# Sums of the second batch by identity matmuls, its inputs fetched a head pair sooner, and the first p_val queued behind the first batch's last o_l

## The chip, the cores and the metric

The kernel runs on one core of one Trainium2 chip, in one launch. The metric is the device time of one execution in microseconds (us), median of the runs shown. TensorE is PE in the profile (its weight loads PEld), VectorE is DVE, ScalarE is ACT, GpSimd is POOL, SyncE is SP; SP issues all DMAs here.

## The reference

Four batches go through attention, a gated convolution block and a mixer block, all in float32. Cut to what matters:

```python
# attention: B, H, S, D = 4, 8, 576, 64; factor 4
q_d = q.reshape(B, H, S // 4, 4, D).mean(axis=3)      # the same for k and v
out_up = np.repeat(softmax(q_d @ k_d.T / 8) @ v_d, 4, axis=2)
out_local = softmax(where(|i - j| < 4, q @ k.T / 8, -1e9)) @ v
x = out_up + out_local                                # (B, S, 512) over the heads
# gated convolution
gate = sigmoid(sum_k conv_w[k] * x shifted by 4 - k positions)
x = (gate * (x @ w_val)) @ w_out
# mixer
u = x + (relu(x.T @ w_tok1) @ w_tok2).T
out = u + relu(u @ w_ch1) @ w_ch2                     # w_ch1: 512 x 1536, w_ch2: 1536 x 512
```

## The kernel before

Everything is held transposed: channels on the 128 partitions, positions along the free axis. A head pair is 128 channels (two heads of 64), so a batch has four head pairs (NHP = 4), and x has four such chunks.

**Attention of a batch** (`attention(b)`) is a generator. For each head pair it runs these steps: `load` (DMAs of q and k into `qk_sb` and of v, four positions apart, into `v4_sb`, which the profile calls v_sb of in_v), `sums` (the sums of four positions: `qk_d` for q and k, `vd` for v), `low_scores` (scores `sc_d` of the sums, and the softmax `e_d`), `loc_scores` (scores `sc_l` of windows of 64 positions, softmax `e_l`), `low_turn` and `low_out` (transposes `pt_d`, products `o_d`, which ACT repeats into `x_f`), `loc_turn` and `loc_out` (transposes `pt_l`, products `o_l`, which DVE adds to `x_f`), and `conv` (the convolution on DVE). There are two buffers for `qk_sb`; one comes free when the `sc_l` matmuls of its head pair are done.

`sums` has two forms. In batch 0, four PE matmuls with the identity as weights add up the four positions in PSUM (each takes every fourth column, 288 of them, in plain float32; the profile records each as two MATMULs), and ACT copies the sum to SBUF. In the other batches one DVE reduction does it.

**The rest of a batch** is `p1(b)`: x is split into a high and a low part (`x_hl`: ACT makes the high part, POOL the low one), every large product is three matmuls (`mm3`, lines 194 to 196: high by high, high by low, low by high). `val` makes `p_val` = x @ w_val, one 128-channel chunk per bank, `outs` makes `p_x`, `transposed` the transposes `x_ps`, then `r_ps`, `p_h` (both tok products) and at last `u_hl`. `c1(b)` makes `g_ps` = u @ w_ch1, and ACT's relu `r_sb` goes to DRAM. `c2` reads it back at the end and makes `p_o` with w_ch2.

The weights come as pairs of 32-bit words and are decoded on the way: three DVE instructions per piece (`decode`, lines 124 to 127, buffers `w64` and `wa`, three each), a high part on ACT and a low one on POOL.

**Order.** Batch 0's attention runs first, with idle matmuls (`busy`, line 108) between its steps. There the framework's scheduler sets the order on all engines. From then on PE's order is written out by hand: `mix` runs `first_products` (p1 and c1 of all batches) and takes a step of the next batch's attention or of a weight's decoding after so many microseconds of planned PE time (`A_AT`: batch 1 from 8 to 59). The other engines' order remains the scheduler's, by program order and priority. Each engine then goes through its own list in order, and waits at the first instruction that isn't ready.

Of the kernel before, what the change touches and what calls it, by code (L numbers as in the profile page):

```python
# [21 lines left out]
NHP = H // 2  # L22
# [52 lines left out]
def kernel(ctx, tc, qk, vw, v4, w_val, conv_w, w_out, w_tok1, w_tok2, w_ch1, w_ch2, out):  # L75
    nc = tc.nc
# [5 lines left out]
    def T(p, shape, dt, tag, bufs, name=None):  # L82
        return p.tile(shape, dt, tag=tag, bufs=bufs, name=name or tag)
# [113 lines left out]


    xf, gate = {}, {}
    LU = [(0, 6), (6, 10)]  # L200

    def load(b, hp):

        early = b == 0 and hp > 1
        t = T(sb, [128, 2, PADW], F32, "uhl" if early else "qk", NUH if early else 2, name="qk_sb")
        nc.sync.dma_start(out=t, in_=qk[b, hp])
        tag, bufs = ("x2r", NX2) if b == 0 and hp > 0 else ("v4", NV4)
        w = T(sb, [72, 4, 2, 128], F32, tag, bufs, name="v4_sb")
        nc.sync.dma_start(out=w, in_=v4[b, hp])
        return {"qk": t, "v4": w, "v": load_v(b, hp) if b == 0 else None}  # L210

    def load_v(b, hp):
        tag, bufs = ("w1", NW1R) if b == 0 and hp > 1 else ("v", NV)
        v = T(sb, [128, NCK // 2, 128], F32, tag, bufs, name="v_sb")
        nc.sync.dma_start(out=v, in_=vw[b, hp])
        return v
# [24 lines left out]
    def attention(b):  # L241
        x_t = xf[b] = [T(sb, [128, CQ * NCK], F32, "xf", NXF, name="x_f32") for _ in range(KC)]
        g_t = gate[b] = [T(sb, [128, S], F32, "gate", NXF, name="gate_sb") for _ in range(KC)]
        hpd = {}
        early = lambda: tc.high_priority(offset=PRI) if b else nullcontext()

        def bank(shape, name):
            if b:
                tag = "as" if name[:2] == "sc" else "ao"
            else:  # L250
                tag = TAG0.get(name, "ao")
            return T(ps, shape, F32, tag, BANKS[tag], name=name)

        def sums(hp):
            d = hpd[hp]
            w = d.pop("v4")
            qk_d = T(sb, [128, 2, SD], F32, "qkd", ND, name="qk_d")
            qd, kd = qk_d[:, 0], qk_d[:, 1]
            qk_4 = d["qk"][:, :, 3:3 + S].rearrange("p i (a r) -> p i a r", r=4)
            if b == 0:  # L260
                p = bank([128, 2, SD], "qk_d")
                for r in range(4):
                    nc.tensor.matmul(p, lhsT=ident, rhs=qk_4[:, :, :, r], start=(r == 0), stop=(r == 3))
                nc.scalar.activation(out=qk_d, in_=p, func=AF.Copy)
            else:
                nc.vector.tensor_reduce(out=qk_d, in_=qk_4, axis=AX.X, op=ALU.add)
            vd = d["vd"] = T(sb, [72, 2, 128], F32, "vd", NVD, name="vd")
            nc.gpsimd.tensor_tensor(out=w[:, 0:2], in0=w[:, 0:2], in1=w[:, 2:4], op=ALU.add)
            nc.gpsimd.tensor_tensor(out=vd, in0=w[:, 0], in1=w[:, 1], op=ALU.add)
            d["qkd"] = qd, kd  # L270

        def low_scores(hp):
            d = hpd[hp]
            qd, kd = d.pop("qkd")
            parts = [bank([72, 2, SD], "sc_d") for _ in range(2)]
            for c in range(2):
                for h, p in enumerate(parts):
                    r0 = 64 * h
                    nc.tensor.matmul(p[:, c, :], lhsT=qd[r0:r0 + 64, c * HD:c * HD + HD],
                                     rhs=kd[r0:r0 + 64, :], start=True, stop=True)  # L280
            e = d["ed"] = T(sb, [72, 4, SD], F32, "e", NE, name="e_d")
            softmax(parts, e, 0.125 / 16.0)

        def low_turn(hp):
            d = hpd[hp]
            e = d.pop("ed")
            ts = d["pd"] = []
            for h in range(2):
                p = bank([72, 2, 2, HD], "pt_d")
                for kc in range(2):  # L290
                    for c in range(2):
                        nc.tensor.transpose(p[:, kc, c, :], e[:, 2 * h + c, kc * HD:kc * HD + HD], ident[0:72, 0:72])
                t = T(sb, [72, 2, 2, HD], F32, "pt", NPT, name="pts_d")
                with early():
                    nc.scalar.activation(out=t, in_=p, func=AF.Copy)
                ts.append(t)
# [15 lines left out]
        def loc_scores(hp):  # L312
            d = hpd[hp]
            qk = d.pop("qk")
            parts = []
            for c0, c1 in LU:
                n = c1 - c0
                p = bank([128, n, WIN], "sc_l")
                nc.tensor.matmul(p.rearrange("p a w -> p (a w)"), lhsT=ident16,
                                 rhs=mask[:, c0:c1, :].rearrange("p a w -> p (a w)"), start=True, stop=False)  # L320
                for c in range(n):
                    o = CQ * (c0 + c)
                    for h in range(2):
                        r0 = 64 * h
                        nc.tensor.matmul(p[r0:r0 + 64, c, :], lhsT=qk[r0:r0 + 64, 0, 3 + o:3 + o + WIN],  # L325
                                         rhs=qk[r0:r0 + 64, 1, o:o + WIN], start=False, stop=(c == n - 1))
                parts.append(p)
            e = d["el"] = T(sb, [128, NCK, WIN], F32, "e", NE, name="e_l")
            softmax(parts, e, 0.125)

        def loc_turn(hp):
            d = hpd[hp]
            e = d.pop("el")
            ts = d["pl"] = []
            for c0, c1 in LU:
                n = (c1 - c0) // 2
# [9 lines left out]
        def loc_out(hp):  # L346
            d = hpd.pop(hp)
            v, ts = d["v"], d["pl"]
            ps_o = [bank([128, NCK // 2, CQ], "o_l") for _ in range(2)]
            for j, t in enumerate(ts):  # L350
                for par in range(2):
                    r0 = 64 * par
                    for h in range(2):
                        nc.tensor.matmul(ps_o[par][64 * h:64 * h + 64, j, :],
                                         lhsT=v[r0:r0 + 64, j, 64 * h:64 * h + 64],
                                         rhs=t[r0:r0 + 64, 64 * h:64 * h + CQ], start=True, stop=True)
            xs = x_t[hp].rearrange("p (j a q) -> p j a q", a=2, q=CQ)
            with early():
                for par in range(2):
                    nc.vector.tensor_tensor(out=xs[:, :, par, :], in0=ps_o[par], in1=xs[:, :, par, :], op=ALU.add)  # L360
# [12 lines left out]
        def sigmoid(s0=0, s1=S):  # L373
            for g in g_t:
                nc.scalar.activation(out=g[:, s0:s1], in_=g[:, s0:s1], func=AF.Sigmoid)

        if b:

            hpd[0] = load(b, 0)
            hpd[0]["v"] = load_v(b, 0)  # L380
            yield
            sums(0)
            for i in range(NHP + 1):
                if i < NHP:
                    low_scores(i)
                    yield
                if i:
                    low_turn(i - 1)
                    yield
                if i < NHP:  # L390
                    loc_scores(i)
                    yield
                if i + 1 < NHP:
                    hpd[i + 1] = load(b, i + 1)
                    sums(i + 1)
                if i:
                    low_out(i - 1)
                    yield
                    loc_turn(i - 1)
                    yield  # L400
                    loc_out(i - 1)
                    conv(i - 1)
                    yield
                if i + 1 < NHP:
                    hpd[i + 1]["v"] = load_v(b, i + 1)
            sigmoid()
            return
# [42 lines left out]
    def hv(hs):  # L450
        return slice(hs * HS, hs * HS + HS)

    def bank(tag, name):
        return T(ps, [128, 512], F32, tag, BANKS[tag], name=name)

    def cxs(p, w, xs, c, ks=range(KC)):
        for k in ks:
            mm3(p[:, 0:HS], [w[k][j][:, c * 128:c * 128 + 128] for j in range(2)],
                [xs[j][:, k] for j in range(2)], k == 0, k == KC - 1)
# [3 lines left out]
    def p1(b):  # L463

        wv, wo, t1, t2 = wt["val"], wt["out"], wt["tok1"], wt["tok2"]
# [9 lines left out]

        def val(hs, c, x, y2):
            p = bank(P1T["p_val"], "p_val")
            cxs(p, wv, x, c)
            with first():
                y = T(sb, [128, HS], F32, "y32", NY, name="y32")  # L480
                nc.vector.tensor_tensor(out=y, in0=p[:, 0:HS], in1=gate[b][c][:, hv(hs)], op=ALU.mult)  # L481
                hi_lo(y, y2[0][:, c], y2[1][:, c], nc.gpsimd if b else nc.vector)
# [24 lines left out]
        x = x_pair(0)  # L507
# [4 lines left out]
        x = x_pair(1)  # L512
# [36 lines left out]
        for hs in range(2):  # L549
            us.append(pair("u", "uhl", NUH))  # L550
            for c in range(KC):
                p = bank(P1T["p_h"], "p_h")
# [170 lines left out]
```

## Time and profile before

| | |
|---|---|
| median of 3 runs | 666.46 us (664.31 to 666.83) |
| the profiled execution: time / span | 664.67 us / 662.8 us |
| PE busy | 622.3 us, 94% of the span |
| DVE, ACT, POOL busy | 339.4, 316.4, 210.0 us |
| mean granted TensorE clock | 0.972 of 2.4 GHz |

Busy time is a share of the whole span. Batch 0's attention fills the first 80 us or so, the second batch's runs beside batch 0's products from about 94 to 190 us, and roughly the last quarter of the span is w_ch2. The granted clock has two levels, 1.2 and 2.4 GHz; a mean between 0.5 and 1 says how long each held.

### The profile page before, as it was taken

The numbers are of one execution on the slowest core, as the hardware profiler recorded it, in microseconds if no ns is written. First come the engines' busy times: TensorE is split into PE (matmuls) and PEld (weight loads), VectorE is DVE, ScalarE is ACT, GpSimd is POOL, SyncE is SP. The second block draws the span as 40 slices with busy tenths as digits, with TensorE's granted clock in tenths as the row PEclk, the third lists the DMA queues.
The fourth block names the chain that finished last, engine by engine and source line by source line (L and its number), as shares of the span: only waits on it lengthen the run. The fifth ranks groups of instructions, "written<-read, shape, count | busy, mean of one in ns | idle before, by whom it ended". The sixth has DMA issues, their size and how long they took to land.

```text
span 662.8 us, 12825 instructions
## 1 busy us (share of the span) xinstructions
PE 622.3 (94%) x4911; PEld 529.6 (80%) x4911; DVE 339.4 (51%) x630; ACT 316.4 (48%) x1044; POOL 210.0 (32%) x242
## 2 busy tenths in 40 slices
PE   8999778897979999999999999999998999999997
PEld 3444477785878988998998999998897888888887
DVE  3679999775686465442344434117635242324232
ACT  1758457485548586546656843324433222222221
POOL 5564655336536422614231323205513000000000
PEclk8999798797979999999999999999999999999999
DMA  7744226623675244784322586565898345454221
GB/s 254 235 143 117 76 81 205 217 75 122 221 244 178 87 150 131 242 245 124 105 72 72 146 255 203 160 195 187 252 355 272 96 144 174 142 176 127 80 74 38
DMA packets 53900, 107.23 MB, mean 162 GB/s; under 512 B 5776, under 2 KB 21392, under 8 KB 53840
## 3 DMA queue, kind: packets, MB, share of 16 engines
q1 hardware_dynamic: 53840, 106.42, 51.1%
q8 instruction: 38, 0.62, 0.4%
q14 instruction: 22, 0.18, 0.1%
HBM read 76.52 MB, written 29.88 MB: 161 GB/s over the span
## 4 chain that ended last, share of the span: by engine, by line
PE 60%; DVE 6%; DMA 5%; ACT 3%; issue 2%; POOL 1%; SPq 0%; DVEq 0%; ACTq 0%
PE p_o L194 7%; PE p_o L196 7%; PE p_o L195 7%; PE g_ps L194 5%; PE g_ps L195 5%; PE g_ps L196 5%; DMA w<-in_w_ch_dram 4%; PE sc_l L325 2%; PE p_x L194 2%; DVE wa L124 2%; PE p_x L195 2%; PE p_x L196 2%; PE p_val L194 2%; PE p_val L196 2%; PE p_val L195 2%
## 5 line engine op out<-in xcount | busy, mean ns | idle before, releaser
L194 PE MATMUL g_ps<-u_hl,w_hl 128*128 128x288 f32 x384 | 117.8, 307 | 0.0
L195 PE MATMUL g_ps<-u_hl,w_hl 128*128 128x288 f32 x384 | 115.0, 299 | 2.1 <-POOL u_hl L444 1.9
L196 PE MATMUL g_ps<-u_hl,w_hl 128*128 128x288 f32 x384 | 113.9, 297 | 0.0
L194 PE MATMUL p_o<-g_hl,ch 128*128 128x512 f32 (+1 forms) x240 | 88.8, 370 | 2.2 <-ACT r_sb L585 2.1
L196 PE MATMUL p_o<-g_hl,ch 128*128 128x512 f32 (+1 forms) x240 | 88.5, 369 | 0.0
L195 PE MATMUL p_o<-g_hl,ch 128*128 128x512 f32 (+1 forms) x240 | 88.5, 369 | 0.0
L443 ACT ACTIVATE g_hl<-r_back 128x512 fp32r<-128x512 f32 (+1 forms) x60 | 35.3, 589 | 109.1 <-PE p_o L196 106.3
L444 DVE TENSOR_TENSOR g_hl<-r_back,g_hl 128x512 fp32r<-128x512 f32 (+1 forms) x60 | 39.4, 658 | 92.8 <-ACT g_hl L443 89.6
L195 PEld LDWEIGHTS g_ps<-u_hl,w_hl 128*128 128x128 f32 x384 | 73.3, 191 | 3.5 <-POOL u_hl L444 3.5
L194 PEld LDWEIGHTS g_ps<-u_hl,w_hl 128*128 128x128 f32 x384 | 73.1, 190 | 3.1 <-issue 1.7
L196 PEld LDWEIGHTS g_ps<-u_hl,w_hl 128*128 128x128 f32 x384 | 73.2, 191 | 0.0
L370 DVE SCALAR_TENSOR_TENSOR gate_sb<-x_f,cw,gate_sb 128x575 f32<-128x575 f32 (+5 forms) x68 | 62.8, 930 | 1.5 <-ACT gate_sb L367 0.5
L585 ACT ACTIVATE r_sb<-g_ps 128x288 f32<-128x288 f32 x96 | 38.2, 406 | 47.0 <-PE g_ps L196 41.2
L124 DVE TENSOR_SCALAR wa<-w 128x256 int32<-128x256 int32 (+2 forms) x76 | 37.1, 499 | 34.8 <-DMA w<-in_w_ch_dram 21.1
L194 PEld LDWEIGHTS p_o<-g_hl,ch 128*128 128x128 f32 x240 | 45.2, 188 | 10.8 <-ACT r_sb L585 3.2
L196 PEld LDWEIGHTS p_o<-g_hl,ch 128*128 128x128 f32 x240 | 45.2, 188 | 7.7
L195 PEld LDWEIGHTS p_o<-g_hl,ch 128*128 128x128 f32 x240 | 45.3, 189 | 7.6
L234 ACT ACTIVATE e_l<-sc_l,mx 128x64 f32<-128x64 f32 x160 | 48.1, 331 | 0.4
L194 PE MATMUL p_x<-y_hl,out_hi 128*128 128x288 f32 x128 | 40.9, 320 | 4.2 <-ACT u_sb L494 3.7
L125 DVE SCALAR_TENSOR_TENSOR wa<-w,wa 128x256 int32<-128x256 int32 (+2 forms) x76 | 44.2, 591 | 1.1
L444 POOL TENSOR_TENSOR x_hl<-x_f,x_hl 128x288 fp32r<-128x288 f32 x32 | 27.7, 877 | 45.5 <-ACT x_hl L443 44.8
L194 PE MATMUL p_val<-x_hl,val_hi 128*128 128x288 f32 x128 | 39.5, 309 | 1.4 <-DVE y L481 0.7
(108 smaller groups left out, 1354.0 us busy)
## 6 DMA issues: line engine op xcount, KB each, us to landing
w_hl<-w_dr SPq DMA_DIRECT2D x36, 512.0 KB, 4.6
r_dr<-r_sb SPq DMA_DIRECT2D x48, 288.0 KB, 4.6
w<-in_w_ch_dram SPq DMA_DIRECT2D x48, 256.0 KB, 3.4
r_back<-r_dr SPq DMA_DIRECT2D x48, 256.0 KB, 3.0
qk_sb<-in_qk_dram SPq DMA_DIRECT2D x16, 589.0 KB, 4.0
w_dr<-w_hl SPq DMA_DIRECT2D x12, 512.0 KB, 3.0
v_sb<-in_vw_dram SPq DMA_DIRECT2D x16, 320.0 KB, 4.0
v_sb<-in_v_dram SPq DMA_DIRECT2D x16, 288.0 KB
```

The lines of the kernel that those rows point to most:

```text
L124: nc.vector.tensor_scalar(a, high, 3, 0x3FFFFFF8, ALU.logical_shift_left, ALU.bitwise_and)
L125: nc.vector.scalar_tensor_tensor(out=a, in0=high, scalar=-0x40000000, in1=a, op0=ALU.bitwise_and, op1=ALU.bitwise_or)
L194: nc.tensor.matmul(out_ap, lhsT=lh, rhs=rh, start=first, stop=False)
L195: nc.tensor.matmul(out_ap, lhsT=lh, rhs=rl, start=False, stop=False)
L196: nc.tensor.matmul(out_ap, lhsT=ll, rhs=rh, start=False, stop=last)
L234: nc.scalar.activation(out=e[:, o, :], in_=p[:, c, :], func=AF.Exp, scale=scale, bias=mx[:, o:o + 1], accum_out=sm[:, o:o + 1])
L325: nc.tensor.matmul(p[r0:r0 + 64, c, :], lhsT=qk[r0:r0 + 64, 0, 3 + o:3 + o + WIN], rhs=qk[r0:r0 + 64, 1, o:o + WIN], start=False, stop=(c ...
L370: nc.vector.scalar_tensor_tensor(out=g[:, t0:s1], in0=x[:, t0 - sh:s1 - sh], scalar=cw[:, hp, k:k + 1], in1=g[:, t0:s1], op0=ALU.mult, op1 ...
L443: nc.scalar.activation(out=hi_ap, in_=src_ap, func=AF.Copy)
L444: lo_eng.tensor_tensor(out=lo_ap, in0=src_ap, in1=hi_ap.bitcast(F32), op=ALU.subtract)
L585: nc.scalar.activation(out=r[:, hv(hs)], in_=p[:, 0:HS], func=AF.Relu)
```

## The change

Three edits. `sums` takes the identity-matmul form for batch 1 too. Batch 1 loads two head pairs before its loop, and then the one after next behind `sums` of the next, where it loaded one ahead. And the first `p_val` chunk of batch 0 gets an order edge on PE: its matmuls are queued behind the last `o_l` matmul of batch 0's attention.

```diff
+    last_pe = [None]
...
-            if b == 0:
+            if b < 2:
                 p = bank([128, 2, SD], "qk_d")
                 for r in range(4):
                     nc.tensor.matmul(p, lhsT=ident, rhs=qk_4[:, :, :, r], start=(r == 0), stop=(r == 3))
                 nc.scalar.activation(out=qk_d, in_=p, func=AF.Copy)
             else:
                 nc.vector.tensor_reduce(out=qk_d, in_=qk_4, axis=AX.X, op=ALU.add)
...
-                        nc.tensor.matmul(ps_o[par][64 * h:64 * h + 64, j, :],
+                        last_pe[0] = nc.tensor.matmul(ps_o[par][64 * h:64 * h + 64, j, :],
...
-            hpd[0] = load(b, 0)
+            ahead = 2 if b == 1 else 1
+            for i in range(ahead):
+                hpd[i] = load(b, i)
...
+                if ahead == 1 and i + 1 < NHP:
+                    hpd[i + 1] = load(b, i + 1)
                 if i + 1 < NHP:
-                    hpd[i + 1] = load(b, i + 1)
                     sums(i + 1)
+                if ahead == 2 and i + 2 < NHP:
+                    hpd[i + 2] = load(b, i + 2)
...
-            cxs(p, wv, x, c)
+            with tc.issue_after(last_pe[0].ins) if b + hs + c == 0 else nullcontext():
+                cxs(p, wv, x, c)
```

What this does to the engines' lists is seen in three places. The first is PE's list at the last head pair of batch 0. Before, the first p_val (12 matmuls for one chunk) stood spread between the attention's steps, one chunk of x at a time:

```order
L292 MATMUL pt_d<-ident,e_d 72x72 x8
L194 MATMUL p_val<-x_hl,val_hi 128x288
L195 MATMUL p_val<-x_hl,val_hi 128x288
L306 MATMUL o_d<-pts_d,vd 64x144
L108 LDWEIGHTS idle
L108 MATMUL idle_ps<-idle 128x512
L196 MATMUL p_val<-x_hl,val_lo 128x288
```

Now the same place reads so:

```order
L293 MATMUL pt_d<-ident,e_d 72x72 x8
L307 MATMUL o_d<-pts_d,vd 64x144
L108 LDWEIGHTS idle
L108 MATMUL idle_ps<-idle 128x512
L108 LDWEIGHTS idle
L108 MATMUL idle_ps<-idle 128x512
```

Nine p_val matmuls (three of the four chunks of x) have left the attention's steps; all twelve follow the last o_l and its idle matmuls.

The second place is PE's list in batch 0's products, where the second batch's first head pair takes its turn. Before:

```order
L196 MATMUL p_x_1101<-y_hl,out_lo 128x288
L279 MATMUL sc_d<-qk_d 72x144 x4
L194 MATMUL p_x_1100<-y_hl,out_hi 128x288
L195 MATMUL p_x_1100<-y_hl,out_hi 128x288
L196 MATMUL p_x_1100<-y_hl,out_lo 128x288
```

Now:

```order
L196 MATMUL p_x_1101<-y_hl,out_lo 128x288
L264 MATMUL qk_d<-qk_sb,ident 128x288 x4
L280 MATMUL sc_d<-qk_d 72x144 x4
L194 MATMUL p_x_1100<-y_hl,out_hi 128x288
L195 MATMUL p_x_1100<-y_hl,out_hi 128x288
```

Four identity matmuls stand right ahead of the scores that read their sum by way of ACT. It is the same for the second head pair (between p_val and x_ps); those of the third and fourth stand ahead of the o_d of the head pair two before, with their scores some 50 matmuls later. The third one's, now (before, o_d followed p_x directly):

```order
L196 MATMUL p_x_1468<-y_hl,out_lo 128x288
L264 MATMUL qk_d<-qk_sb,ident 128x288 x4
L307 MATMUL o_d<-pts_d,vd 64x144 x4
L194 MATMUL p_x_1467<-y_hl,out_hi 128x288
L195 MATMUL p_x_1467<-y_hl,out_hi 128x288
```

Here o_d, and the p_x that follow it, wait for four more matmuls of PE's own, and nothing reads the sum at once.

The third place is SP's list, where the second batch's third head pair is fetched between the pieces of w_ch1. Before:

```order
L121 DMA w_1659<-in_w_ch_dram 128x2x256
L206 DMA qk_sb<-in_qk_dram 128x1178
L166 DMA w_dr<-w_hl 128x1024
L121 DMA w_1667<-in_w_ch_dram 128x2x256
L121 DMA w_1677<-in_w_ch_dram 128x2x256
```

Now:

```order
L121 DMA w_1678<-in_w_ch_dram 128x2x256
L121 DMA w_1686<-in_w_ch_dram 128x2x256
L121 DMA w_1696<-in_w_ch_dram 128x2x256
L207 DMA qk_sb<-in_qk_dram 128x1178
L166 DMA w_dr<-w_hl 128x1024 x2
```

Both lists have five pieces of w_ch1 up to the first row shown; the fetch of qk_sb, earlier in the program, has moved two pieces of w_ch1 later in SP's list.

## Rows read from the trace of the kernel before

**Rows 1.** The page's first part: busy time, share of the span, instructions.

```profile
PE 622.3 (94%) x4911; PEld 529.6 (80%) x4911; DVE 339.4 (51%) x630; ACT 316.4 (48%) x1044; POOL 210.0 (32%) x242
```

**Rows 2.** Stretches: length, busy (instructions) by engine, granted clock, DMA share, GB/s.

```profile
100.00:120.00 20.00, 17.20 (x176) 14.69 (x175) 19.22 (x43) 12.60 (x62) 10.28 (x12) 0.91 0.69 220
120.00:140.00 20.00, 18.27 (x165) 15.54 (x166) 14.78 (x24) 12.40 (x44) 4.11 (x5) 0.83 0.44 129
140.00:160.00 20.00, 16.00 (x147) 13.29 (x146) 12.44 (x21) 14.58 (x46) 13.44 (x13) 0.97 0.37 127
160.00:180.00 20.00, 17.83 (x186) 15.77 (x186) 10.96 (x21) 11.53 (x51) 10.27 (x12) 0.86 0.55 189
180.00:220.00 40.00, 35.86 (x344) 33.41 (x343) 28.90 (x59) 23.90 (x83) 20.39 (x23) 0.91 0.61 200
220.00:400.00 180.00, 177.40 (x1766) 162.06 (x1765) 78.50 (x141) 111.84 (x386) 57.97 (x64) 1.00 0.50 150
```

**Rows 3.** PE's timeline, 96 to 190 us: its main waits, idle time in brackets.

```profile
100.07 0.32 PE L319 MATMUL sc_l<-mask,ident 128*128 128x384 bf16 x1 [2.18 <-ACT e_d L234]
106.77 0.46 PE L279 MATMUL sc_d<-qk_d 64*72 64x144 f32 x2 [1.07 <-DVE wa L124]
108.28 0.71 PE L279 MATMUL sc_d<-qk_d 64*72 64x144 f32 x6 [1.05 <-ACT e_l L234]
121.73 0.61 PE L194 MATMUL p_x<-y_hl,out_hi 128*128 128x288 f32 x1 [2.34 <-ACT u_sb L494]
154.80 0.40 PE L195 MATMUL g_ps<-u_hl,w_hl 128*128 128x288 f32 x1 [0.81 <-POOL u_hl L444]
160.76 0.48 PE L319 MATMUL sc_l<-mask,ident 128*128 128x384 bf16 x1 [2.64 <-ACT e_d L234]
187.18 1.60 PE L354 MATMUL o_l<-pts_l,v_sb 64*64 64x58 f32 x40 [3.62 <-ACT pts_l L343]
```

**Rows 4.** Batch 0, head of the program: PE and ACT at pts_d; DVE's restart.

```profile
69.62 0.51 PE L306 MATMUL o_d<-pts_d,vd 72*64 72x144 f32 x2 [1.38 <-ACT pts_d L295]
...
68.50 0.78 ACT L375 ACTIVATE gate_sb<-gate_sb 128x288 f32<-128x288 f32 x2 [3.54 <-DVE gate_sb L370]
...
61.11 1.02 DVE L124 TENSOR_SCALAR wa<-w 128x256 int32<-128x256 int32 x2 [1.01 <-POOL out_lo L131]
```

**Rows 5.** Three stretches of the same kind as rows 2.

```profile
61.11:89.63 28.52, 23.19 (x194) 16.42 (x194) 28.38 (x50) 14.91 (x40) 16.55 (x17) 0.88 0.28 78
121.73:127.14 5.41, 5.41 (x24) 5.39 (x24) 3.97 (x5) 1.88 (x12) 3.24 (x3) 0.50 0.74 224
100.00:104.00 4.00, 3.93 (x47) 3.22 (x47) 3.60 (x9) 1.70 (x9) 3.04 (x4) 0.58 0.45 133
```

**Rows 6.** Tile qk_d: the DVE reductions; durations in ns, min/median/max.

```profile
L266 DVE TENSOR_REDUCE qk_d<-qk_sb x12: 1340/1350/1355, 53.3 to 328.8; 128x288 f32<-128x1152 f32 x12
```

**Rows 7.** PE's timeline in batch 0: identity matmuls, and the scores that follow them.

```profile
5.84 4.28 PE L263 MATMUL qk_d<-qk_sb,ident 128*128 128x288 f32 x8 [1.05 <-DMA qk_sb<-in_qk_dram]
...
45.14 1.26 PE L263 MATMUL qk_d<-qk_sb,ident 128*128 128x288 f32 x2
...
46.98 0.71 PE L279 MATMUL sc_d<-qk_d 64*72 64x144 f32 x8
```

**Rows 8.** The chain that ended last: two of its pieces (start, us, what).

```profile
165.74 0.13 PE g_ps L194
...
169.00 0.41 ACT r_sb L585
```

**Rows 9.** ACT's timeline at 121 us: the copies ahead of PE's wait there.

```profile
120.64 0.67 ACT L309 ACTIVATE x_f<-o_d 128x576 f32<-128x576 f32 x1
...
121.23 0.75 ACT L494 ACTIVATE u_sb<-p_x 128x288 f32<-128x288 f32 x2
```

**Rows 10.** POOL's timeline, 142 to 158 us.

```profile
142.09 0.74 POOL L269 TENSOR_TENSOR vd<-v_sb 72x256 f32<-72x256 f32 x1 [1.02 <-PE o_d L306]
...
153.45 4.09 POOL L444 TENSOR_TENSOR u_hl<-u_sb,u_hl 128x288 fp32r<-128x288 f32 x4
```

## The prediction

> **What bounds the kernel now.** I read the page's busy shares first [rows 1]: PE works 94% of the span, no other engine over 51%. That says where the time is, not what this change is worth, since the edits touch 45 to 190 us only. So I cut the span into stretches next [rows 2]. The reader is to see two regimes. From 220 us PE is busy 177.4 of 180 us at the full clock: whatever PE has lost or gained by then stays in the end time, one for one. From 100 to 220 us PE is idle for 14.8 of 120 us (20 less 17.20, 18.27, 16.00 and 17.83, and 40 less 35.86), and the clock's mean there is 0.83 to 0.97, so some stretches run at 1.2 GHz. This is where added PE work might hide. PE's own timeline [rows 3] names the waits there: seven make up 13.7 us, and each stands at one instruction of the second batch's attention or beside it. The question is whether the identity matmuls stand ahead of those waits and fill them, or stand elsewhere and add to them.
>
> **First p_val behind the last o_l.** Before, PE held o_d of the last head pair back behind a p_val. But that o_d then waited still longer, for ACT's pts_d, which stood behind a sigmoid that waited 3.54 us for DVE [rows 4]. DVE is what counts in the head: from 61.11 to 89.63 us it is busy 28.38 of 28.52 us [rows 5], its list there is the same after the change, and the last y_hl that p_x needs is at its end. Without the p_val, PE is only idle sooner. Two reductions of the second batch, 1.35 us each [rows 6], leave DVE ahead of 61 us, but DVE waited for POOL there (1.01 us, rows 4), and POOL's work followed from ACT's. I count a gain of 0.3 us, one decode step that no longer stands ahead of a reciprocal. The bounds are 0 and, if the whole wait went, 1.0.
>
> **Sums by identity matmuls, the price of one.** The trace has the same instructions in batch 0: one head pair's eight records take 4.28 us back to back at the full clock [rows 7]. Four head pairs make 17.1 us of PE. What DVE saves, four times 1.35 us [rows 6], doesn't come off this: it counts only where PE waits for DVE. Where the scores follow the sum directly, PE also waits for ACT's copy: in batch 0 the last sum matmul ends at 45.14 + 1.26 = 46.40 and sc_d starts at 46.98, 0.58 us later, and the stretch between is filled with idle matmuls that the new places don't have.
>
> The Trainium skill prices such a matmul differently: "FP8 and Floating Point Precision", section "TensorE Precision Notes", has true float32 take four passes through the array. The chain has a one-pass matmul of 288 columns every 0.13 us [rows 8]; four of them are 0.53 us, and four matmuls 2.1 us a head pair, 8.5 us in all. The rows of the operation itself say 4.28, twice as much; the rows decide, and what the rule would give is a rival below.
>
> **First head pair.** Its four matmuls stand ahead of sc_d in the middle of p_x, where PE had no wait. They add 4.28 + 0.58 = 4.9 us. The wait of 2.18 us at 100.07 [rows 3] isn't covered: it is for e_d, which follows sc_d through DVE, an ACT table load and four exponentials, and sc_d is itself late by these 4.9. Bounds: 4.3 (copy hidden) and 6 (ACT behind other casts when the sum is ready).
>
> **Second head pair.** Here they stand where PE waited for sc_d's banks, 1.07 and 1.05 us [rows 3]. From the start of the first of these (106.77 - 1.07 = 105.70) to the end of sc_d (108.28 + 0.71 = 108.99) PE took 3.3 us. Now it takes 4.28 + 0.58, and 0.71 for sc_d, 5.6 us. So it adds 2.3 us; 4.9 if the bank wait comes back behind the sum.
>
> **Third head pair.** The matmuls stand ahead of o_d, and nobody reads the sum at once, so no copy is exposed. Their 4.28 us give ACT time: before, o_d's copy x_f started at 120.64 behind six exponentials, and the u_sb copy behind it at 121.23 set PE's wait of 2.34 us [rows 9, 3]. Now the exponentials run under the sum. After o_d, ACT needs about 0.67 and some 0.1 for x_f and 0.4 for u_sb, and PE has 0.8 us of p_x to do: a wait of some 0.4 is left, 1.9 less. What followed that wait ran at the low clock: 121.73 to 127.14 at 0.50 [rows 5], 5.4 us for work of 2.7. If PE doesn't stop, I expect that the clock doesn't fall: 2.7 us back. The sum is 4.28 - 1.9 - 2.7 = -0.3. Bounds: -0.5, and +4.3 if the wait stays.
>
> **Fourth head pair.** The matmuls stand ahead of the second head pair's o_d. POOL's vd waits for that o_d (142.09), a fetch of v waits for vd, and POOL then works through to the last u_hl (153.45 + 4.09 = 157.54), for which PE waits [rows 10, 3]. So the 4.28 us go into POOL's chain whole. In return POOL's list now has one u_hl (about 0.8 us) ahead of the fetched v, under its transfer: 0.7 back. It adds 3.6; bounds 2.9 and 4.3.
>
> **The earlier fetch** I cost at nothing: qk_sb of the third head pair still waits for the sc_l of the first to free its buffer, and PE has two p_val chunks, the second head pair's scores and most of a p_x to do before it sums. In SP's list it now stands behind two more pieces of w_ch1, which can only help the decoding. Beyond 158 us the engines' lists are the same as before, so I carry the lateness through: 160.76 and 187.18 wait for work that itself follows from PE (r_sb at 169.00 after g_ps, rows 8).
>
> **Sum.** -0.3 + 4.9 + 2.3 - 0.3 + 3.6 = +10.2 us. On the profiled execution's 664.67 us (span 662.8) that is 674.9; on the median of the runs, 666.46, it is 676.7, as the profiled one was among the faster. I forecast 675.5 us, slower by 1.4%. Its own range, from the bounds and a clock fall more or less (some 2.7), is 671 to 680.
>
> **Rivals.**
>
> *The cover at the third head pair fails*: PE still waits at p_x, and the clock still falls. For it: ACT's list now puts all ten exponentials and the sum's copy ahead of x_f. Against: 4.28 us are more than those ten take once their maxima are there. It costs 4.6 to 4.9 more: about 680.
>
> *The lateness is absorbed at the third head pair's o_l.* If ACT's pts_l comes by DVE's decoding of w_ch1 and not by PE, the wait of 3.62 us at 187.18 vanishes, with the low clock behind it (180 to 220 us has a mean of 0.91, up to 3.6 us): 7.2 back, about 668. For it: DVE is relieved, SP fetches two pieces sooner. Against: the chain runs through g_ps and r_sb at 169.00.
>
> *Faster: PE comes late to every wait.* This one ends on the other side. The side engines run ahead while PE does sums, so that the waits at 100.07, 160.76 and 187.18 all go (8.4 us), with the low clock behind them: 100 to 104 has 0.58 [rows 5], 1.7 us; 160 to 180 has 0.86 [rows 2], 2.8; 180 to 220 up to 3.6. Together 16.5, so -6.3: 658 to 660. It decides where more than 10.2 of these 16.5 vanish. For it: each of these stalls is short and beside the second batch's attention. Against: 100.07 waits on sc_d, which the sum delays.
>
> *The sum costs half*, 8.5 us instead of 17.1, so +1.6: 666 to 668. Against it: all four groups of batch 0 run at the same pace, with the same tiles and the same stride. The four-pass rule of the Trainium skill's page cited above is this rival.
>
> **How the numbers follow.** Forecast 0.55; the cover fails 0.15; absorbed at o_l 0.13; faster 0.10; the sum costs half 0.02; still slower by several waits that I don't see 0.05. The range takes in the first two, the absorbed and the half case: 666 to 682, 0.85 less the edges. Half a percent, 3.3 us, is about what a measurement of this kernel can tell from no change: faster is under 663.1, slower over 669.8. Slower: 0.55 + 0.15 + 0.05 = 0.75; the same 0.13 + 0.02 = 0.15; faster 0.10.
>
> **What would show it.** In the profile after: 16 more identity matmuls of batch 1 from about 94 us at 4.28 us a head pair, at full clock; sc_l of the first head pair some 4.6 us later than 100.07 and still after a wait of about 2; no wait of 2 us at p_x in the third head pair's place, and no clock of 0.5 behind it; the POOL chain ending some 10 us later than 157.5; eight reductions of qk_d in place of twelve. The head up to 94 us should be the same within 1 us. Wrong would be: p_x starting 2 us or more sooner than 89.6 (then p_val's place was worth more), an end of the POOL chain under 162 us, or waits at 187 us that are gone.

## The result

The changed kernel takes 675.95 us (median of 4 runs, 673.53 to 677.37), the kernel before 665.9 us on the same chip. The ratio is 1.015, with an interval of 1.0113 to 1.0186: slower by 10.0 us, where 675.5 us was forecast. The profiled execution took 675.86 us, its span 674.0, 11.2 more than before; the places below are read from that one.

The page's first part for the kernel after, to be held against [rows 1]:

```profile
PE 635.6 (94%) x4943; PEld 533.9 (79%) x4943; DVE 331.3 (49%) x626; ACT 318.7 (47%) x1048; POOL 212.4 (32%) x242
```

PE has 32 more instructions (16 matmuls, two records each) and 13.3 us more of busy time; DVE has lost 8.1 us, at 51% of the span before. The stretches of the kernel after, with the columns of [rows 2]:

```profile
100.00:120.00 20.00, 17.72 (x137) 13.53 (x133) 14.93 (x39) 14.33 (x61) 7.96 (x9) 0.91 0.57 189
120.00:140.00 20.00, 19.87 (x188) 15.10 (x187) 10.14 (x24) 8.95 (x38) 6.38 (x6) 1.00 0.51 158
140.00:160.00 20.00, 19.42 (x172) 13.66 (x171) 10.82 (x19) 14.76 (x51) 6.60 (x7) 1.00 0.23 74
160.00:180.00 20.00, 15.03 (x122) 12.94 (x122) 10.09 (x19) 11.69 (x41) 9.35 (x11) 0.83 0.39 132
```

From 120 to 160 us PE hardly waits (0.7 us in all) and doesn't fall to 1.2 GHz; before, it was idle there for 5.7 of 40 us at 0.83 and 0.97. Part of that has only moved: from 160 to 180 us PE is now idle for 5.0 us at 0.83, where it was 2.2 at 0.86. Over the whole of 100 to 180 us the idle time falls from 10.7 to 8.0 us, and that gain is spent on the sums. Next PE's own timeline, first three marks of the kernel before that [rows 3] lack (the p_x that opens the stretch, pt_d and o_l around the third head pair's place):

```profile
91.38 0.40 PE L194 MATMUL p_x<-y_hl,out_hi 128*128 128x288 f32 x1 [0.76 <-ACT u_sb L494]
111.02 0.66 PE L292 MATMUL pt_d<-ident,e_d 72*72 72x72 f32 x8
128.47 0.81 PE L354 MATMUL o_l<-pts_l,v_sb 64*64 64x58 f32 x40
```

and the same engine in the kernel after:

```profile
91.83 0.40 PE L194 MATMUL p_x<-y_hl,out_hi 128*128 128x288 f32 x1 [0.77 <-ACT u_sb L501]
94.96 4.22 PE L264 MATMUL qk_d<-qk_sb,ident 128*128 128x288 f32 x8
99.68 0.71 PE L280 MATMUL sc_d<-qk_d 64*72 64x144 f32 x8 [0.50 <-ACT qk_d L265]
104.76 0.32 PE L320 MATMUL sc_l<-mask,ident 128*128 128x384 bf16 x1 [1.78 <-ACT e_d L235]
114.94 0.71 PE L280 MATMUL sc_d<-qk_d 64*72 64x144 f32 x8 [0.50 <-ACT qk_d L265]
117.68 0.66 PE L293 MATMUL pt_d<-ident,e_d 72*72 72x72 f32 x8
124.26 4.22 PE L264 MATMUL qk_d<-qk_sb,ident 128*128 128x288 f32 x8
129.05 0.40 PE L194 MATMUL p_x<-y_hl,out_hi 128*128 128x288 f32 x1
134.17 0.81 PE L355 MATMUL o_l<-pts_l,v_sb 64*64 64x58 f32 x40
153.85 0.44 PE L340 MATMUL pt_l<-ident,e_l 128*128 128x128 f32 x2 [0.58 <-ACT pts_l L344]
162.35 0.40 PE L194 MATMUL p_h<-tok_hl,r_hl 128*128 128x288 f32 x1 [1.49 <-DVE u_sb L565]
171.16 0.48 PE L320 MATMUL sc_l<-mask,ident 128*128 128x384 bf16 x1 [2.71 <-ACT e_d L235]
198.02 1.60 PE L355 MATMUL o_l<-pts_l,v_sb 64*64 64x58 f32 x40 [3.62 <-ACT pts_l L344]
```

Read as lateness against before: +0.45 us at the first p_x (91.83 against 91.38); +4.69 at sc_l (against 100.07, [rows 3]), so 4.24 for the first head pair; +6.66 at the end of the second sc_d (115.65 against 108.99), 1.97 for the second; from pt_d to o_l 16.49 us where it was 17.45, so -0.96 for the third; +10.40 at the next sc_l (against 160.76), 4.70 for the fourth; +10.84 at o_l (against 187.18), +11.2 at the end. The waits at 171 and 198 us stand as they did at 161 and 187. Two waits are new: 0.58 us at pt_l, and 1.49 at p_h, for DVE's u_sb. What DVE and POOL did there:

```profile
158.84 3.08 DVE L366 TENSOR_SCALAR gate_sb<-x_f,cw 128x576 f32<-128x576 f32 x1
161.85 0.44 DVE L565 TENSOR_TENSOR u_sb<-p_h,u_sb 128x288 f32<-128x288 f32 x1
```

```profile
157.33 1.26 POOL L240 TENSOR_TENSOR e_l<-e_l,sm 128x640 f32<-128x640 f32 x1
158.55 2.31 POOL L450 TENSOR_TENSOR u_hl<-u_sb,u_hl 128x288 fp32r<-128x288 f32 x3
160.83 0.78 POOL L450 TENSOR_TENSOR x_hl<-x_f,x_hl 128x288 fp32r<-128x288 f32 x1
161.58 1.00 POOL L450 TENSOR_TENSOR u_hl<-u_sb,u_hl 128x288 fp32r<-128x288 f32 x1
165.40 2.46 POOL L450 TENSOR_TENSOR u_hl<-u_sb,u_hl 128x288 fp32r<-128x288 f32 x2 [1.54 <-ACT u_hl L449]
```

The convolution's first tap, a DVE TENSOR_SCALAR, lasted 3.08 us. POOL ran back to back beside it, and the tap ended at 161.92, 0.3 us behind POOL's x_hl; the u_hl that follows took 1.00 us, where the three ahead took 2.31 together. The group of the twelve taps has a median of 0.52:

```profile
L366 DVE TENSOR_SCALAR gate_sb<-x_f,cw x12: 507/521/3085, 135.9 to 410.8; 128x576 f32<-128x576 f32 x12
```

u_sb stood behind it, PE waited for u_sb, and POOL's last two u_hl, made from later u_sb, came after an idle 1.54 us: POOL's chain ended at 167.86, 10.3 us later than in [rows 10].

All this holds one execution against one other, and these two are the ends of what the fourteen kernels of this document show. From the p_x of the first mark to the sc_l of the fourth head pair the three kernels with all four sums on DVE took 69.38 us (the kernel before), 70.70 and 70.94; the five with all four on PE at the price of 4.22 us took between 77.11 and 79.33 (the kernel after). By the means that is 7.8 us; between the two profiles it is 9.95.

### The profile page after: what moved, and what is told of

Same layout as the page of the kernel before. It is cut to its first block, busy times and chain, and to the rows that moved or that the text cites. A ratio compares the mean times of both kernels' runs of the same rounds, so it can differ in the third digit from the quotient of the medians.

```text
span 674.0 us, 12890 instructions
## 1 busy us (share of the span) xinstructions
PE 635.6 (94%) x4943; PEld 533.9 (79%) x4943; DVE 331.3 (49%) x626; ACT 318.7 (47%) x1048; POOL 212.4 (32%) x242
## 4 chain that ended last, share of the span: by engine, by line
PE 74%; DVE 11%; DMA 7%; ACT 5%; issue 2%; SPq 1%; POOL 1%; DVEq 0%; ACTq 0%
PE p_o L194 7%; PE p_o L196 7%; PE p_o L195 7%; PE g_ps L194 5%; DMA w<-in_w_ch_dram 5%; PE g_ps L196 5%; PE g_ps L195 5%; PE qk_d L264 4%; PE sc_l L326 4%; DVE gate_sb L371 3%; PE p_x L194 2%; PE p_val L194 2%; PE p_x L196 2%; PE p_x L195 2%; PE p_val L196 2%
## 5 line engine op out<-in xcount | busy, mean ns | idle before, releaser
L194 PEld LDWEIGHTS p_o<-g_hl,ch 128*128 128x128 f32 x240 | 45.2, 188 | 11.2 <-ACT r_sb L592 3.6
L124 DVE TENSOR_SCALAR wa<-w 128x256 int32<-128x256 int32 (+2 forms) x76 | 32.1, 433 | 36.0 <-DMA w<-in_w_ch_dram 23.1
L125 DVE SCALAR_TENSOR_TENSOR wa<-w,wa 128x256 int32<-128x256 int32 (+2 forms) x76 | 42.4, 567 | 1.3
```

The lines of the kernel that those rows point to most:

```text
L124: nc.vector.tensor_scalar(a, high, 3, 0x3FFFFFF8, ALU.logical_shift_left, ALU.bitwise_and)
L125: nc.vector.scalar_tensor_tensor(out=a, in0=high, scalar=-0x40000000, in1=a, op0=ALU.bitwise_and, op1=ALU.bitwise_or)
L194: nc.tensor.matmul(out_ap, lhsT=lh, rhs=rh, start=first, stop=False)
```

## Experiments

My theory was the prediction's: the sums alone make the change, in four terms that add up, and the edits of order are worth nothing. The rivals were that fetch or edge carry part of the time, that lateness is absorbed at later waits, and that the price of a sum is another. Each ratio below is against the kernel before on the same chip.

**The two halves of the change.** First the sums without the rest:

```diff
-            if b == 0:
+            if b < 2:
```

> The kernel before with the four sums of the second batch as identity matmuls, and neither the order edge nor the earlier fetch. My theory: the sums are the whole change, the two edits of order cost and gain nothing. At the places: sc_l of the first head pair about 4.3 us later than 100.07 with a wait of 1.8 left, sc_d of the second ending 6.3 us later than 108.99, the last u_hl of POOL about 10 us later than 157.54; the time 9.5 to 11 us over the kernel before. Rival: part of the lateness after is the fetch's (POOL's new wait of 5.2 us at vd, the 1.49 us at p_h); then this kernel is only 5 to 8 us slower and the p_h wait is gone.

673.17 us, ratio 1.0114 (1.0084 to 1.0144). The wait at p_h (1.55) is that of the kernel after, and POOL's last u_hl ends at 164.32, 6.8 us later than in [rows 10] where I had expected about 10; counted from the third head pair's o_l it is as in the kernel after. Less than forecast, 7.6 us for 9.5 to 11, though its interval overlaps that of the kernel after. In its profile the first head pair cost only 3.5 us:

```profile
90.39 0.40 PE L194 MATMUL p_x<-y_hl,out_hi 128*128 128x288 f32 x1 [0.77 <-ACT u_sb L494]
102.63 0.32 PE L319 MATMUL sc_l<-mask,ident 128*128 128x384 bf16 x1 [1.03 <-ACT e_d L234]
```

12.24 us between these two, where the kernel after takes 12.93 and that before 8.69; the wait is 1.03 for 1.78. The second head pair, from this sc_l to the end of sc_d, took 9.44 us at a clock of 1.00, where the kernel after takes 10.89 at 0.84. Then the other half:

```diff
-            if b < 2:
+            if b == 0:
```

> The kernel after with the second batch's sums back on DVE: the order edge of the first p_val and the earlier fetch alone. My theory: within 1 us of the kernel before; p_x of batch 0 starts 0 to 0.5 us later than 89.59 as in the kernel after. Rival 1: the edge gains and the sums hide it, then 1 to 3 us faster. Rival 2: the fetch collides with the decoding of w_ch1, then 2 to 5 us slower, with new waits between 100 and 160 us.

666.34 us, ratio 1.0008 (0.9989 to 1.0027): the two order edits are worth nothing together. A wait has moved all the same: in DVE's list the first reduction of the third batch now stands ahead of r_hl (in the kernel before, behind it) and waits for its qk_sb, and r_hl is what PE waits 2.68 us for at p_h. The kernel with the second head pair alone, below, has the same order without the fetch, so this is not the fetch's own. The end doesn't show it.

```profile
142.20 1.35 DVE L267 TENSOR_REDUCE qk_d<-qk_sb 128x288 f32<-128x1152 f32 x1 [3.76 <-DMA qk_sb<-in_qk_dram]
```

**One head pair at a time**, the others on DVE (here the third; hp is 0, 1 and 3 in the other three):

```diff
-            if b == 0:
+            if b == 0 or (b, hp) == (1, 2):
```

> The kernel before with the identity matmuls for the third head pair of the second batch alone; the other three stay on DVE. My theory (the matmuls fill a wait of 2.34 us and keep the clock up where 5.4 us ran at 0.50): no wait over 0.6 us at the p_x of about 122 to 126 us, a clock of 1.00 there, and everything behind it 0.5 to 1.2 us sooner than before; the time 0 to 1.5 us less, not to be told from no change. Rival: in the kernel after the wait went because the two head pairs ahead had made PE late, not because of the matmuls; then a wait of over 1 us stands at p_x still, the clock falls to about 0.5 behind it, and the time is 2 to 4.3 us more.

669.1 us, ratio 1.0044 (1.0025 to 1.0062), slower where I expected no change. Yet the place itself did as in the kernel after:

```profile
114.07 0.67 PE L292 MATMUL pt_d<-ident,e_d 72*72 72x72 f32 x8
130.56 0.81 PE L354 MATMUL o_l<-pts_l,v_sb 64*64 64x58 f32 x40
155.14 0.61 PE L194 MATMUL p_h<-tok_hl,r_hl 128*128 128x288 f32 x1 [2.48 <-DVE u_sb L558]
```

```profile
120.00:140.00 20.00, 19.87 (x186) 14.71 (x184) 12.60 (x24) 11.84 (x46) 4.57 (x5) 1.00 0.50 144
```

16.49 us from pt_d to o_l once more, no wait at p_x, the clock at 1.00: the cover needs no lateness of the first two pairs. But the 17.45 us that it is held against are those of one execution. In the five other kernels that leave this sum on DVE, with the same PE instructions between pt_d and o_l, that stretch took 14.15 to 15.91 us; PE waited at p_x there too (1.85 to 2.04), and the clock stayed at 1.00 in three of them and had a mean of 0.89 in two. The kernel before, and the one with the fourth head pair alone:

```profile
111.02:128.47 17.45, 15.11 (x125) 13.83 (x123) 14.92 (x28) 9.39 (x44) 8.06 (x9) 0.80 0.74 233
112.94:127.14 14.20, 12.32 (x125) 11.05 (x123) 11.07 (x23) 8.59 (x40) 6.38 (x8) 1.00 0.64 208
```

Against those five the sum costs 0.6 to 2.3 us at its own place. A further wait comes at p_h, with the same DVE instruction, here 4.07 us beside POOL's run (150.14 to 154.41 without a gap):

```profile
150.65 4.07 DVE L365 TENSOR_SCALAR gate_sb<-x_f,cw 128x576 f32<-128x576 f32 x1
```

> The kernel before with the identity matmuls for the first head pair of the second batch alone. My theory: 4.3 to 4.7 us more at sc_l (100.07 before, wait of 1.8 left), and all of it carried through to the end, since the waits at 160 and 187 us follow from PE itself: 4 to 5 us slower. Rival: lateness is absorbed at later waits (2.34 us at p_x of 121.73, 2.64 at sc_l of 160.76, 3.62 at o_l of 187.18) as long as it is small, and only the sum of several runs over; then under 2 us slower, with these waits shorter.

674.35 us, ratio 1.0116 (1.0061 to 1.0170). From the p_x at 92.14 to sc_l at 105.28 it takes 13.14 us for 8.69 before, 4.45 more, as forecast; but the total is some 8 us. The tap took 4.62 us, and PE waited 3.03 at p_h (and 1.75 at r_ps, for DVE's x_hl). My theory lacked that; the rival's "under 2 us" is out. The profiled execution, 677.33 us, was the slowest of its four.

> The kernel before with the identity matmuls for the second head pair of the second batch alone. My theory: they stand in the place of two bank waits of 1.07 and 1.05 us; sc_d ends 2.0 to 2.3 us later than 108.99, and the time is 1.5 to 3 us more. If the waits come back behind the sum: 4.3 to 4.9 more. If absorbed at later waits: 0.

668.24 us, ratio 1.0043 (1.0014 to 1.0072), 2.4 us more: my theory's size. The tap took 1.13 us there.

> The kernel before with the identity matmuls for the fourth head pair of the second batch alone. My theory: they stand ahead of the o_d for which POOL's vd waits, POOL's last u_hl ends 3.6 to 4.6 us later than 157.54, and the time is 3.5 to 5 us more; a new wait of over 1 us at p_h shows that it is this head pair's own. Rival: the new waits in the kernel after (0.58 at pt_l, 1.49 at p_h) come from the lateness of the head pairs ahead of it; then POOL's chain ends 2.9 to 3.6 us later and p_h doesn't wait.

670.62 us, ratio 1.0078 (1.0055 to 1.0101), 4.75 us more. POOL ends at 161.74, 4.2 later than in [rows 10]; p_h waits 1.55 and the tap takes 3.14 us, without any lateness of the pairs ahead. So the new wait comes with this head pair alone, as my theory had it; but it comes with the first or the third alone too, so it isn't this head pair's own.

The four alone make 1.16 + 0.43 + 0.44 + 0.78 = 2.8%, all four together 1.1%. So the terms of the ends don't add up. The wait for u_sb at p_h is met by three of the four and by all four together (3.03, 2.48 and 1.55 us alone, 1.55 together); counted once, it would make 5.5 of the 11 us, if it is paid at the end; the control below puts that in doubt. The second head pair's wait at p_h is another, for r_hl:

```profile
148.11 0.61 PE L194 MATMUL p_h<-tok_hl,r_hl 128*128 128x288 f32 x1 [1.95 <-DVE r_hl L544]
```

The rest isn't settled.

**The price of a sum.** The identity matmuls read adjacent columns, so that other positions are summed:

```diff
+            qk_c = d["qk"][:, :, 3:3 + S].rearrange("p i (r a) -> p i a r", r=4) if b else qk_4
...
-                    nc.tensor.matmul(p, lhsT=ident, rhs=qk_4[:, :, :, r], start=(r == 0), stop=(r == 3))
+                    nc.tensor.matmul(p, lhsT=ident, rhs=qk_c[:, :, :, r], start=(r == 0), stop=(r == 3))
```

> The kernel after, but the second batch's identity matmuls read four blocks of adjacent columns in place of every fourth column, which sums up other positions; all else is the same. It asks for the price: 4.2 us a head pair now. If the stride of the columns makes it, the nearest row of adjacent float32 columns is sc_d (0.71 us for eight records of 144 columns, so 0.18 for one of 288): eight records take 1.4 us a head pair, and the terms become about 1.9, 0, 0 (-2.7 to +1.4) and 1.2, the time some 3 to 4 us over the kernel before. If four passes were the price, 2.1 us a head pair and 4 to 5 us over. Rival: the stride is nothing, and the price comes from the type and the 128 rows; then 4.2 us a head pair and 10 us over, as now.

669.87 us, ratio 1.0072 (1.0042 to 1.0102), 4.3 us more in place of 10. The price is 2.10 us a head pair, not 1.4 and not 4.2:

```profile
94.01 2.10 PE L265 MATMUL qk_d<-qk_sb,ident 128*128 128x288 f32 x8
97.40 0.71 PE L281 MATMUL sc_d<-qk_d 64*72 64x144 f32 x8 [1.29 <-ACT qk_d L266]
```

So 0.53 us a matmul, four times the one-pass 0.13 of [rows 8], and every fourth column doubles it. The four passes of the Trainium skill ("FP8 and Floating Point Precision", section "TensorE Precision Notes"), which the prediction set against the row, hold where columns are adjacent. What they leave out is the stride: in the Trainium skill's "SBUF — State Buffer", section "Door 1: The DMA port swizzle (why `[64,N]` ≈ `[32,N]`)", SBUF has lines of 16 bytes and wants two reads in a line for the full rate; four float32 columns are 16 bytes. The trace fits that, with 4.22 against 2.10; that the lines are the cause isn't shown, as no other stride was run.

**The third batch too**, where PE is full:

```diff
-            if b < 2:
+            if b < 3:
```

> The kernel after with the identity form for the third batch as well, beside products during which PE was busy 98.6% of its time (220 to 400 us before). My theory: there nothing hides them; 4.2 us a head pair, and up to 0.5 for the exposed copy: 17 to 19 us over the kernel after, 27 to 30 over the kernel before. Rival: DVE's freed time (4 x 1.35 us) or fuller use of PE gives some back; then under 14 us over the kernel after.

690.57 us, ratio 1.0377 (1.0328 to 1.0425): 14.6 us over the kernel after, between the two. Ahead of these sums, the 3.62 us that PE waited at o_l are gone, and 3.31 stand at pt_d, where the kernel after waits 1.41:

```profile
185.85 0.84 PE L293 MATMUL pt_d<-ident,e_d 72*72 72x72 f32 x8 [3.31 <-DVE x_f L361]
194.21 1.01 PE L355 MATMUL o_l<-pts_l,v_sb 64*64 64x58 f32 x40
```

That o_l starts 7.03 us later than in [rows 3], 3.8 less than in the kernel after. Of these 3.8 us 1.5 are there from the start of the stretch (p_x at 90.34), and 1.1 come from p_h, where PE waits 0.41 for 1.49; the rest I didn't take apart (the lists of DVE and ACT differ there). From that o_l to the end (span 688.6, 25.8 over before) 18.8 us are added: four sums of 4.22, a copy of 0.50 behind the first and the second, which the scores follow directly, and 0.9 more. The price is paid whole.

**The slow tap.** Three kernels ask whether it is the cause of the wait at p_h. ACT makes it in the first, one instruction moved:

```diff
-            if b:
+            if b and (b, hp) != (1, 1):
                 nc.vector.tensor_scalar(g[:, s0:s1], x[:, s0:s1], cw[:, hp, TAPS - 1:TAPS], None, ALU.mult)
```

> The kernel after with one instruction moved: the first tap of the convolution of the second batch's second head pair (gate_sb, TENSOR_SCALAR on DVE, 3.08 us at 158.84 in the kernel after, where eleven others take 0.5 to 1.5) is made by ACT. My theory: that DVE instruction is held while POOL works through u_hl and x_hl back to back, u_sb behind it comes late, and PE waits 1.49 us for it at p_h, which also sends POOL's last two u_hl late (they wait 1.54 us). On ACT the wait at p_h goes, POOL's chain ends 1.5 to 2 us sooner, and the time is 1.5 to 2.5 us under the kernel after, so 8 to 9 us over the kernel before. Rival 1: POOL's chain is long by itself; p_h's wait goes and comes back at g_ps, no gain. Rival 2: the tap on ACT stands ahead of POOL's u_hl casts and delays them by its 0.76 us; 0 to 1 us slower than the kernel after.

676.34 us, ratio 1.0135 (1.0105 to 1.0166): no gain. The wait at p_h is gone, and what stands behind it shows why nothing came of it:

```profile
157.88 3.62 DVE L371 SCALAR_TENSOR_TENSOR gate_sb<-x_f,cw,gate_sb 128x575 f32<-128x575 f32 x1
```

```profile
163.28 0.37 PE L194 MATMUL g_ps<-u_hl,w_hl 128*128 128x288 f32 x1 [1.30 <-DVE u_sb L565]
```

The second tap, 0.98 us at 162.22 in the kernel after, is held in the first one's place, and PE waits some instructions later. Rival 1 was right on the time; that the instruction after the moved one is held as well, neither had said.

> The kernel of the third head pair alone with the same tap made by ACT. There the DVE instruction took 4.07 us and PE waited 2.48 us at p_h, with a low clock behind it. My theory: both go, and with them the 3 us by which that kernel was slower than the sum of its places; what the third head pair gives by itself is 1 us, so 1 to 2 us faster than the kernel before (663.5 to 664.8). Rival: the wait comes from u_sb's other work, then 2 to 4 us slower than before, as without the edit.

667.27 us, ratio 1.0006 (0.9983 to 1.0028): 0.9 us over the kernel before, where it was 3.5 without the edit, and not the 1 to 2 us faster that I expected. The second tap took 4.61 us, and g_ps waited 2.28: the time fell though the hold stayed.

> The kernel before with the same tap made by ACT, as a control: there it took 1.03 us on DVE and PE didn't wait for it. My theory: within 0.7 us of the kernel before. Rival: the move is worth something or costs something by itself (ACT's casts later, DVE free sooner), then 1 us or more either way.

666.18 us, ratio 0.9997 (0.9972 to 1.0022), as expected. But its trace has the hold as well, without any sum on PE:

```profile
151.39 4.66 DVE L370 SCALAR_TENSOR_TENSOR gate_sb<-x_f,cw,gate_sb 128x575 f32<-128x575 f32 x1
157.82 0.37 PE L194 MATMUL g_ps<-u_hl,w_hl 128*128 128x288 f32 x1 [2.34 <-DVE u_sb L558]
```

So a hold of 4.66 us and a wait of 2.34 behind it stand in the trace of a kernel that is no slower than the kernel before. Each kernel has one trace, so whether all its executions have the hold isn't known; that the hold makes the other kernels slower is not shown.

The last kernel leaves the tap and takes POOL's run away:

```diff
-hi_lo(uu, us[hs][0][:, c], us[hs][1][:, c], nc.gpsimd)
+hi_lo(uu, us[hs][0][:, c], us[hs][1][:, c], nc.vector if b + hs == 0 and c else nc.gpsimd)
```

> The kernel after with three low-part casts of u_hl (batch 0, first half, chunks 1 to 3; 2.31 us of POOL's list from 158.55 on) made by DVE ahead of the convolution's first tap, so that POOL isn't busy without a gap while DVE comes to that tap; PE, ACT and SP keep their lists. My theory (the DVE instruction can't run while POOL runs back to back): the tap takes 0.5 to 1.1 us in place of 3.08, although DVE has 1.4 us more to do; PE's wait at p_h falls from 1.49 to about 0.5 or less, POOL's last u_hl ends 1 to 2 us sooner than 167.86, counted from the same start, and the time is 0.5 to 2 us under the kernel after. Rival: the tap is slow for another reason (the memory that it reads, DMA traffic); then it takes 3 us still, p_h waits 2.5 us or more, and the time is 1 us more.

672.03 us, ratio 1.0096 (1.0076 to 1.0116): 7.0 us over the kernel before, where the kernel after is 10.0 over (the two intervals just touch). That is somewhat more than I expected; at the sc_l of the fourth head pair the profile has 2.2 of it. Only 0.74 of these lie where the edit acts, between the third head pair's o_l and that sc_l; 1.45 are the second head pair's stretch, 9.44 us at a clock of 1.00 as with the sums alone.

```profile
155.95 2.52 DVE L450 TENSOR_TENSOR u_hl<-u_sb,u_hl 128x288 fp32r<-128x288 f32 x2
159.50 0.50 DVE L366 TENSOR_SCALAR gate_sb<-x_f,cw 128x576 f32<-128x576 f32 x1
```

```profile
156.69 1.47 POOL L240 TENSOR_TENSOR e_l<-e_l,sm 128x640 f32<-128x640 f32 x1
163.49 2.45 POOL L450 TENSOR_TENSOR u_hl<-u_sb,u_hl 128x288 fp32r<-128x288 f32 x2 [0.26 <-ACT u_hl L449]
```

With POOL idle from 158.16 to 159.76 the tap takes 0.50 us, on the same tile. Two of the DVE casts, of which the one ahead at 155.13 took 0.45, now take 2.52 and end at 158.47, just behind POOL's e_l: held too. p_h waits 0.93 us, POOL ends at 165.94.

That a DVE instruction can be held while POOL works is shown. In the ten traces in which POOL works beside the tap, the tap ends 0.31 to 0.34 us behind the end of one of POOL's instructions, with no gap of POOL's in the record. Behind which one isn't settled, and it isn't a matter of who comes first alone: in the kernel before, the tap came 0.57 us into POOL's e_l and got through behind it; with the third head pair alone it came 0.51 us into the same e_l, and four more instructions of POOL passed before it got through.

```profile
147.91 1.26 POOL L239 TENSOR_TENSOR e_l<-e_l,sm 128x640 f32<-128x640 f32 x1
148.48 1.03 DVE L365 TENSOR_SCALAR gate_sb<-x_f,cw 128x576 f32<-128x576 f32 x1
149.13 3.59 POOL L444 TENSOR_TENSOR u_hl<-u_sb,u_hl 128x288 fp32r<-128x288 f32 x3
```

```profile
150.14 1.26 POOL L239 TENSOR_TENSOR e_l<-e_l,sm 128x640 f32<-128x640 f32 x1
```

That it is a lock on a shared port is the Trainium skill's word for it ("SBUF — State Buffer", section "Who interferes with whom": `tensor_scalar` can contend with GpSimd, as do DVE instructions with two SBUF inputs, and the loser "fully blocks"). The runs agree for three kinds of instruction: 3.08, 3.62 and 2.52 us. Where the page has the lock for the length of one instruction, the tap of 3.08 us let four of POOL's pass.

No version beat the kernel before.

## Why the prediction was right, point by point

- **Head, -0.3 predicted, +0.45 measured.** Neither is a finding. Over all fourteen kernels the p_x at 91.38 starts between 90.34 and 93.64 us; its mean is 91.4 with the edge (six kernels) and 91.9 without (eight). The edge is worth nothing that can be told.
- **First head pair, 4.9 predicted, 4.24 measured at sc_l.** The sum and the copy came as said (4.22 and 0.50). The wait for e_d stayed, but at 1.78 for 2.18, which I had taken as fixed.
- **Second, 2.3 predicted, 1.97 measured.** The bank waits were filled as said.
- **Third, -0.3 predicted, -0.96 measured.** Right in both halves, the wait filled and the clock kept; the wait of 0.4 that I had left over didn't come. The same -0.96 in the kernel with this pair alone. But the 2.7 us of low clock that I counted back belong to one execution of the kernel before: against the five other kernels with this sum on DVE (14.15 to 15.91 us) the same 16.49 are 0.6 to 2.3 more.
- **Fourth, 3.6 predicted, 4.70 measured, above its bounds.** The step that failed is "In return POOL's list now has one u_hl ... ahead of the fetched v, under its transfer: 0.7 back". The u_hl did go there (154.61, ahead of v_sb at 156.09), and behind the e_l that follows POOL was 9.42 us late, where vd had been 9.96 late. Then it was lost again. POOL's chain was no longer set by the fetched v: its last two u_hl waited 1.54 us for casts of a u_sb that stands behind the held tap in DVE's list. I had read [rows 10] for the order on POOL alone, and not what DVE does beside it. How much of the 1.1 us is the hold stays open: POOL's wait of 1.54 is also there in the kernel of the order edits, where the tap took 1.13 us, and the kernel before took the least of all for this stretch, 32.29 us, where the six others with this sum on DVE took 34.05 to 38.20.
- **Behind 158 us, nothing predicted, +0.8 measured** in the one profile. The waits at 160.76 and 187.18 were carried through as said.
- **The sum**, +10.2 predicted, +10.0 by the medians. The errors (+0.75, -0.66, -0.33, -0.66, +1.1, +0.8) nearly cancel; single terms were good to about 1 us in this pair of executions. That the sum came within 0.2 us is luck in part: by the ends, the four alone are 8.5, 2.4, 3.5 and 4.8 us for 4.9, 2.3, -0.3 and 3.6, and the sums alone are 7.6. The prediction also gives two ranges, 671 to 680 and 666 to 682; the measured time lies in both.
- **Rivals.** The cover held; nothing was absorbed at 187; PE wasn't made faster by coming late (the waits at sc_l and o_l moved with it); the sum didn't cost half, and the adjacent columns show why that rival was near: half is the price without the stride.

## What to carry to other kernels

A reduction moved to a full PE is worth its price only where it fills a wait that something else sets. Of these four the second and the third did so in part, and none paid dependably: the third gained 1 us against one execution of the kernel before and lost 0.6 to 2.3 against five other kernels. So read a wait, and the clock fall behind it, from more than one execution before counting it as a gain. Read the price of a matmul from a row with the same access pattern, since a stride over the columns alone doubled it. And when work shifts by a few us against POOL, look at what DVE runs beside it: an instruction of half a microsecond can take three, and moving it only hands the hold to the next one. What that costs at the end has to be measured; one kernel here had the hold and was no slower.

## What the runs showed of the hardware

- A float32 identity matmul of 288 columns takes 0.53 us with adjacent columns and 1.05 with every fourth (2.10 and 4.22 us for four).
- A DVE TENSOR_SCALAR of 128x576 takes 0.52 us alone and 1.03 to 4.62 us beside POOL. Either engine can be the one that is held: in the kernel before, DVE got its turn after 0.5 us, and the three u_hl of POOL behind it took 3.59 us where they take 2.31 in the kernel after.
